# AFNO block on one core: the second DFT in products of 64 rows, the inverse on quarters of the array, the remainder evacuated once a chunk and moved by DMA

## The chip, the core and the metric

The kernel runs on one core of a Trainium2 chip. The metric is the device time of one execution in microseconds; times here are in microseconds where no other unit stands.

## What is computed

A block of 4096 positions and 640 channels: adaptive layer norm, a spectral mixer (AFNO) with residual, adaptive layer norm, a gated feed-forward layer with residual. The change concerns the mixer alone:

```python
Xf = jnp.fft.rfft2(x, axes=(1, 2))                   # x: (1, 1, 4096, 640)
z = Xf.reshape(B, H, Wf, NB, BS)                     # NB = 4 blocks of BS = 160 channels
hr = zr @ w1[0] - zi @ w1[1] + b1[0]                 # per block; einsum in the source
hi = zi @ w1[0] + zr @ w1[1] + b1[1]
hr = hr * (hr > 0); hi = hi * (hi > 0)
or_ = hr @ w2[0] - hi @ w2[1] + b2[0]
oi_ = hi @ w2[0] + hr @ w2[1] + b2[1]
...                                                  # soft shrink of both with lam = 0.01
return jnp.fft.irfft2(or_ + 1j * oi_, s=(H, W), axes=(1, 2))
```

## The kernel before

The transform of length 4096 is split into 128 x 32 (N1 x N2). A first DFT over N1 (`dft_a`, line 439) runs over eight pieces of the input, and its results are written to DRAM (`s1`, `write_s1`, line 355). The frequencies are then worked through in eight chunks `ch` (`NCH`, in the order `ORDER`), each of 512 frequencies in four groups `j`. A chunk is loaded by `load_g` (lines 308 and 311; the first chunk partly by `move_g`, line 316) into `gs[ch]`, its twiddled second DFT is `tb`.

For each chunk there are five second DFTs, `stage_b(ch, t)` (line 600): t = 0 to 3 for the first 128 channels of the four blocks, t = 4 for the remaining 32 channels of all four together (the remainder). `evac_b` takes a result from PSUM into a high and a low part `z` (ACT line 607, DVE line 608); `evac_rh` and `evac_rl` take the remainder into `rz`, 32 rows at a time (ACT line 630, DVE line 640). `stage_l1(ch, b)` (lines 661 and 674) is the first mixing layer of block b, `stage_l2` (line 711) the second, into `tts`. `move_x` (line 731) regroups `tts` by DMA into `xx`, `shrink_parts` (lines 737 and 738) and `shrink` are the soft shrink, `shrink_high` (line 752) and `shrink_low` (line 757) split it, and `stage_i` (lines 768 to 770) is the inverse of the second DFT, whose result is evacuated at line 771 and written to `s2` in DRAM by POOL's queue (line 772). The last chunk's inverse is apart (`inverse_last`, line 825), in f32 on 64 rows.

Matmuls with parts are fp32r in three products (high by high, low by high, high by low); `stage_b`, `dft_a`, `inverse_last` and the sums over `ones` are f32, and each of these products has two records in the trace.

The order is written out by hand (`manual_schedule`): what stands first in the program is issued first on its engine. The chunks run in 32 steps `p = 4 * ch + b`; step p has `stage_l1(p)`, one or two `stage_b`, `stage_l2(p - 1)`, `stage_i(p - 7)` and the elementwise work around them. A step with b = 1 has the remainder of the next chunk. `nc.sync` is the DMA queue of SP, in order; it carries the writes to `s1`, `load_g`, `load_tb`, the constants `idn`, `tx`, `bx`, the `move_x` and the loads for the modulation sums (`mod_load`). PSUM has eight banks: `p1`, `p2`, `p3` in pairs and `bank0(i)`, two single ones. Behind the chunks come `first_mm` (lines 983 to 988) and the feed-forward layer.

```python
for b, tag in ((0, None), (4, None), (1, "p2")):      # before the first step
    stage_b(0, b, tag)
...
for b in range(2):
    evac_b(0, b)
    evac_r(0, b)
```

Of the kernel before, what the change touches and what calls it, by code (L numbers as in the profile page):

```python
# [13 lines left out]
P = 128  # L14
# [32 lines left out]
def constants():  # L47
# [8 lines left out]
    fa = np.zeros((N1, 128))  # L56
# [30 lines left out]
    rows = lambda a: a.reshape(a.shape[0], 4, 8, 4, -1).transpose(0, 2, 3, 1, 4).reshape(a.shape[0], 128, -1)  # L87
    tb = rows(tb.transpose(0, 3, 1, 2, 4, 5, 6)).reshape(8, 4, 128, 128)[ORDER].reshape(32, 128, 128)
# [24 lines left out]
    bm = bm.reshape(2, 128, 128)  # L113
    bi = bm[1].reshape(2, 64, 128)

    bx = np.tile(bm[1].reshape(2, 64, 128).transpose(1, 0, 2), (2, 1, 1)).reshape(128, 256)
    bmh, bml = _hl(bm)
    bm = np.stack([bmh, bml], axis=1)
    bm = np.ascontiguousarray(bm.transpose(2, 0, 1, 3)).reshape(128, 2 * 2 * 128)
# [12 lines left out]
    for n in range(4):  # L132
        for h in range(2):
            for r in range(2):
                for i in range(2):
                    m = 4 * (4 * ORDER[-1] + 2 * h + i)
                    ge[64 * i:64 * i + 64, n, 256 * h + 128 * r:256 * h + 128 * r + 128] = (
                        bi[r].reshape(64, 4, 32)[:, :, n] @ ga[n, m:m + 4])
        ge[:, n, 512:] = ga[n]
# [18 lines left out]
def layouts(given):  # L158
    out = {}
    for n in ("A_w1", "A_w2"):  # L160
        w = given[n].transpose(2, 0, 1, 3)
        rows = [w[128:160, ::1 - 2 * (q % 2)] for q in range(4)]
        out[n] = np.ascontiguousarray(np.stack([w[0:128], np.concatenate(rows)]))
# [10 lines left out]
def body(tc, x, w1, b1, w2, b2, wg, wu, wd, c, wm, k_fa, k_tb, k_tx, k_bm, k_bx, k_ga, k_ge, k_id, out, dbg=None):  # L174
# [27 lines left out]
    with ExitStack() as top:  # L202
# [3 lines left out]
        def bank0(i, shape, name):  # L206
            return ps.tile(shape, F32, tag=f"b{i % 2}", bufs=1, name=name)
# [30 lines left out]
        with ExitStack() as af:  # L238
# [4 lines left out]
            bm = wp.tile([P, 2, 2, 128], F32R, name="bm")  # L243
            tx = wp.tile([P, 2], F32, name="tx")
            lp = af.enter_context(tc.tile_pool(name="lp", bufs=1))
            fa = lp.tile([P, 128], F32, name="fa")
# [9 lines left out]
            def prep_weights(raw, wa, wb, wc, split):  # L256
# [11 lines left out]
                for o in range(2):  # L268
                    for oh, ol, n, src in parts(o):
# [6 lines left out]
                                 (wc, h, l, rr[:, o, :, e], 1.0 if o else sgn[:, 0:1])]  # L276
# [19 lines left out]
            def load_tb(ch):  # L296
                tb = lp.tile([P, 4, 128], F32, tag="tb", bufs=2, name=f"tb{ch}")
                nc.sync.dma_start(tb, k_tb[:, 4 * ch:4 * ch + 4])
                tbs[ch] = tb


            def load_g(ch, us=None):
# [3 lines left out]
                src = s1[f].rearrange("(u v) (q e j) d -> e u (v q) (j d)", u=4, e=e, q=4)[ch % e]  # L306
                if us is None:
                    nc.sync.dma_start(gs[ch].rearrange("p j d -> p (j d)"), src.rearrange("u r d -> r u d"))
                else:
                    for u in us:  # L310
                        nc.sync.dma_start(gs[ch][u:P:4].rearrange("p j d -> p (j d)"), src[u])


            def move_g(ch, t, i, dma):
                p = 64 * (t % 2) + 16 * i + t // 2
                dma.dma_start(gs[ch][p:p + 13:4], xas[t][64 * ch:64 * ch + 64:4, i])
# [23 lines left out]
            with tc.tile_pool(name="sp", bufs=1) as sp:  # L340
# [91 lines left out]
                def dft_a(t):  # L432

                    xnr = xas[t].rearrange("p a (b e) -> p a b e", b=NB)
                    for n, i in enumerate((0, 1, 2, 3, 4) if t < 7 else (4, 0, 1, 2, 3)):
                        j = 5 * t + n
                        pa = (bank0(j // 4, [P, 512], f"pa{t}_{i}") if j % 4 == 0
                              else ps.tile([P, 512], F32, tag=f"p{j % 4}", name=f"pa{t}_{i}"))
                        mm(pa, fa, xnr[:, i, :, 0:128] if i < 4 else xnr[:, :, :, 128:160], start=True, stop=True)
# [15 lines left out]
                for t in range(8):  # L455
# [5 lines left out]
                    if t == 6:  # L461

                        prep1 = prep_weights(raws[1], w1a, w1b, w1c, True)
# [34 lines left out]
            load_g(1, range(4))  # L498
# [23 lines left out]
            prep2 = prep_weights(raws[2], w2a, w2b, w2c, False)  # L522
# [64 lines left out]
            pbs = {}  # L587
# [3 lines left out]
            def width(ch):  # L591
                return 258 if ch == CE else 256

            def stage_b(ch, t, tag=None):
                g, tb = gs[ch], tbs[ch]
                pb = (ps.tile([P, 2, 256], F32, tag=tag, name=f"pb{ch}_{t}") if tag else
                      bank0(1 if t == 4 else 0, [P, 2, 256], f"pb{ch}_{t}"))
                col = slice(128 * t, 128 * t + 128)
                for j in range(4):
                    mm(pb[:, :, 64 * j:64 * j + 64], g[:, j, col], tb[:, j, :], start=True, stop=True)  # L600
                pbs[ch, t] = pb

            def evac_b(ch, t):
                pb = pbs[ch, t]
                z = lp.tile([P, 2, 2, 258], F32R, tag="z", bufs=4, name=f"z{ch}_{t}")
                zs[ch, t] = z
                act.activation(z[:, 0, :, 0:256], pb, AF.Identity, scale=ca1[:, t:t + 1])
                dve.scalar_tensor_tensor(z[:, 1, :, 0:256], pb, ca1[:, t:t + 1],
                                         f32(z[:, 0, :, 0:256]), op0=OP.mult, op1=OP.subtract)
                if ch == CE:  # L610
                    pool.tensor_copy(z[:, 0, :, 0:257:256], f32(edge[:, 0, t]))
                    pool.tensor_copy(z[:, 1, :, 0:257:256], f32(edge[:, 1, t]))
                    pool.tensor_copy(z[:, :, :, 257], zero[:, 0, 0])


            def evac_r(ch, b, part=None):
                if part != 1:
                    evac_rh(ch, b)
                if part != 0:
                    evac_rl(ch, b)  # L620
# [1918 lines left out]
```

## Time and profile before

| | |
|---|---|
| three runs, median (lowest to highest) | 1415.19 (1413.05 to 1418.73) |
| span of the profiled execution | 1409.5 |
| its own time beside the span | not given; the median of the runs is 5.7 above the span |
| input, layer norm, first DFT | to about 56 |
| chunks | about 56 to 306 |
| feed-forward layer | about 306 to the end |
| granted clock of TensorE | 1.00 in all stretches asked for |

A row of the time line has the start, the length, the engine, the line, the operation with its tiles, and how many equal instructions it merges; in square brackets is the idle time of the engine ahead of it and what ended it. `PEld` is TensorE's weight load, `SPq` the issuing of DMAs by SP. A row of a group has the count, the busy time, the mean of one in ns, and the idle time ahead. `64*128` is the part of the array that a matmul uses, rows by columns.

### The profile page before, as it was taken

The numbers are of one execution on the slowest core, as the hardware profiler recorded it, in microseconds if no ns is written. First come the engines' busy times: TensorE is split into PE (matmuls) and PEld (weight loads), VectorE is DVE, ScalarE is ACT, GpSimd is POOL, SyncE is SP. The second block draws the span as 40 slices with busy tenths as digits, with TensorE's granted clock in tenths as the row PEclk, the third lists the DMA queues.
The fourth block names the chain that finished last, engine by engine and source line by source line (L and its number), as shares of the span: only waits on it lengthen the run. The fifth ranks groups of instructions, "written<-read, shape, count | busy, mean of one in ns | idle before, by whom it ended". The sixth has DMA issues, their size and how long they took to land. (4 is left out here: it accounts for less than half of the span.)

```text
span 1409.5 us, 23754 instructions
## 1 busy us (share of the span) xinstructions
PE 1382.5 (98%) x8410; PEld 1310.7 (93%) x8410; DVE 1067.8 (76%) x1861; ACT 765.0 (54%) x1542; POOL 604.6 (43%) x683
## 2 busy tenths in 40 slices
PE   6899999999999999999999999999999999999998
PEld 2599999967999889899999999999999999999998
DVE  8889888889888888649787668678678757375644
ACT  6879999755555554436454345546164624262341
POOL 5700200157766594326445534447153624042241
PEclk9999999999999999999999999999999999999999
DMA  9876466675998897898877998696998668956634
GB/s 371 310 244 211 157 196 193 203 232 170 327 353 308 308 335 263 293 368 308 308 225 281 375 330 288 236 326 230 375 330 309 217 218 282 350 194 217 199 115 149
DMA packets 171016, 377.34 MB, mean 268 GB/s; under 512 B 22193, under 2 KB 81649, under 8 KB 168882
## 3 DMA queue, kind: packets, MB, share of 16 engines
q1 hardware_dynamic: 161794, 359.28, 73.6%
q0 software_dynamic: 6800, 13.93, 3.1%
q10 hardware_dynamic: 2304, 2.62, 0.5%
q8 instruction: 66, 1.08, 0.3%
q14 instruction: 52, 0.43, 0.1%
HBM read 269.48 MB, written 96.80 MB: 260 GB/s over the span
## 5 line engine op out<-in xcount | busy, mean ns | idle before, releaser
L1442 DVE TENSOR_TENSOR wb<-r,wb 128x768 fp32r<-128x768 f32 (+3 forms) x170 | 170.4, 1013 | 13.5 <-ACT wb L1435 13.3
L2050 PE MATMUL pw<-h,wt 128*128 128x384 f32 x412 | 139.3, 338 | 0.6 <-ACT s_y L2069 0.6
L2052 PE MATMUL pw<-h,wt 128*128 128x384 f32 x412 | 138.3, 336 | 0.0
L2051 PE MATMUL pw<-h,wt 128*128 128x384 f32 x412 | 138.1, 335 | 0.0
L1435 ACT ACTIVATE wb<-r 128x768 fp32r<-128x768 f32 (+3 forms) x168 | 104.5, 639 | 56.3 <-PE pw L2063 41.7
L2351 PE MATMUL pc<-wq,L 128*128 128x320 f32 x846 | 132.7, 309 | 0.9 <-DMA wq<-wqd 0.9
L2110 POOL TENSOR_TENSOR sg<-s_x,sg 128x384 f32<-128x384 f32 x24 | 30.0, 1250 | 234.5 <-DVE s_x L2076 234.5
L2351 PEld LDWEIGHTS pc<-wq,L 128*128 128x128 f32 x846 | 126.3, 188 | 1.1 <-DVE x L2308 1.1
L2130 DVE TENSOR_TENSOR L<-sg,L 128x384 fp32r<-128x384 f32 x144 | 101.0, 725 | 27.7 <-ACT L L2126 27.2
L2069 ACT ACTIVATE s_x<-pw 128x384 f32<-128x384 f32 x52 | 25.6, 492 | 164.2 <-PE pw L2052 162.3
L2050 PE MATMUL pw<-h,wb 128*128 128x384 f32 x312 | 105.0, 336 | 0.0
L2051 PE MATMUL pw<-h,wb 128*128 128x384 f32 x312 | 104.4, 335 | 0.0
L2052 PE MATMUL pw<-h,wb 128*128 128x384 f32 x312 | 104.4, 335 | 0.0
L2121 POOL TENSOR_TENSOR sg<-sg,sg 128x384 f32<-128x384 f32 x72 | 91.9, 1276 | 23.4 <-DVE L L2130 20.0
L1973 PE MATMUL pg<-ht,wb 128*128 128x512 f32 x260 | 101.8, 392 | 0.0
L2351 PE MATMUL pe<-wq,L 128*128 128x320 f32 x648 | 101.7, 309 | 0.0
L1974 PE MATMUL pg<-ht,wb 128*128 128x512 f32 x260 | 101.3, 390 | 0.0
L1975 PE MATMUL pg<-ht,wb 128*128 128x512 f32 x260 | 101.2, 389 | 0.0
L2267 PE MATMUL pd<-wq,a 128*128 128x320 f32 x632 | 96.8, 310 | 0.0
L2351 PEld LDWEIGHTS pe<-wq,L 128*128 128x128 f32 x648 | 96.6, 188 | 0.0
L2267 PEld LDWEIGHTS pd<-wq,a 128*128 128x128 f32 x632 | 93.5, 188 | 0.5
L772 POOL DMA_DIRECT2D s<-co x28 | 15.7, 559 | 175.9 <-ACT co L771 175.9
(317 smaller groups left out, 3914.1 us busy)
## 6 DMA issues: line engine op xcount, KB each, us to landing
wq<-wqd SPq DMA_DIRECT2D x83, 640.0 KB, 6.1
wt<-td SPq DMA_DIRECT2D x103, 512.0 KB, 5.4
hs<-ho SPq DMA_DIRECT2D x52, 512.0 KB, 5.2
h<-hs SPq DMA_DIRECT2D x32, 768.0 KB, 7.9
td<-wt SPq DMA_DIRECT2D x25, 512.0 KB, 6.3
r<-in_B_w_gate_dram SPq DMA_DIRECT2D x24, 384.0 KB, 4.4
r<-in_B_w_up_dram SPq DMA_DIRECT2D x24, 384.0 KB, 4.3
xx<-tt SPq DMA_DIRECT2D x56, 160.0 KB, 3.3
```

The costliest lines, as they stand in the source:

```text
L1435: def high(ks, e=slice(0, c), copy=lambda o, i: act.activation(o, i, AF.Copy)):
L1442: dve.tensor_tensor(wbs[t, n][:, 1, ks, e], raw[t, n][:, ks, e], f32(wbs[t, n][:, 0, ks, e]), op=OP.subtract)
L1973: mm(b, wh, hh, start=(kk == 0), stop=False)
L1974: mm(b, wh, hl, start=False, stop=False)
L1975: mm(b, wl, hh, start=False, stop=(kk == 4))
L2050: mm(b, w(0, kp), a[:, kp, 0], start=start and kp == 0, stop=False, skip_group_check=not start)
L2051: mm(b, w(0, kp), a[:, kp, 1], start=False, stop=False, skip_group_check=not start)
L2052: mm(b, w(1, kp), a[:, kp, 0], start=False, stop=kp == 1, skip_group_check=not start)
L2121: pool.tensor_tensor(o, x, y, op=op)
L2130: dve.tensor_tensor(o[:, 1], raws[j], f32(o[:, 0]), op=OP.subtract)
L2267: mm(b[:, :320], l, m, start=start and i == 0, stop=stop and i == len(s) - 1)
L2351: mm(o[:, :320], ls[q][:, x, k], w[:, q, y], start=start and q == 0 and n == 0, stop=q == 1 and n == 2, skip_group_check=not start)
```

## The change

`stage_b` no longer multiplies all 128 rows by a matrix of 128 columns, half of it zeros. The rows of `gs` are ordered so that one frequency of each pair lies in rows 0 to 63 and the other in 64 to 127, and each group has two products of 64 rows with 64 columns, one for each half, which write to two banks of PSUM (`bb`, one tile of two banks that `bank0` now hands out too). The remainder (t = 4) is evacuated whole by two ACT and two DVE instructions into a tile `zr`, and `move_r` moves it by four DMAs on SP's queue into `rz`. `stage_i` is in f32 without splitting, as four products of 64 rows and 64 columns, each on a quarter of the array; it stands at p - 6, and its result is written by two DMAs of POOL instead of one. `move_x` needs one DMA for each tile instead of two, `load_g` always four. The load of `bm` moves from POOL's queue to SP's. In the first step the products of `z` stand ahead of those of `rz`.

```diff
+        bb = ps.tile([P, 2, 512], F32, tag="bb", bufs=1, name="bb")
-        def bank0(i, shape, name):
-            return ps.tile(shape, F32, tag=f"b{i % 2}", bufs=1, name=name)
+        def bank0(i):
+            return bb[:, i % 2]
...
-            def stage_b(ch, t, tag=None):
+            def stage_b(ch, t, two=None):
                 g, tb = gs[ch], tbs[ch]
-                pb = (ps.tile([P, 2, 256], F32, tag=tag, name=f"pb{ch}_{t}") if tag else
-                      bank0(1 if t == 4 else 0, [P, 2, 256], f"pb{ch}_{t}"))
+                out = [two[u] if two else bb[:, u] for u in range(2)]
+                out = [o[:, 0:256].rearrange("p (r e) -> p r e", r=2) for o in out]
                 col = slice(128 * t, 128 * t + 128)
                 for j in range(4):
-                    mm(pb[:, :, 64 * j:64 * j + 64], g[:, j, col], tb[:, j, :], start=True, stop=True)
+                    for u in range(2):
+                        k = slice(64 * u, 64 * u + 64)
+                        mm(out[u][:, :, 32 * j:32 * j + 32], g[k, j, col], tb[k, j, :], start=True, stop=True)
...
+            def evac_b(ch, t, two=None):
...
+                if t == 4:
+                    cuts = [(bb[:, :, 128 * r:128 * r + 128], slice(0, 2), r) for r in range(2)]
...
+                for pv, u, r in cuts:
+                    zh, zl = (v[:, u] if r is None else v[:, u, r, cols] for v in zv)
+                    act.activation(zh, pv, AF.Identity, scale=ca1[:, t:t + 1])
+                    dve.scalar_tensor_tensor(zl, pv, ca1[:, t:t + 1], f32(zh), op0=OP.mult, op1=OP.subtract)
...
+            def move_r(ch):
+                rzs[ch] = hp.tile([P, NB, 260], F32R, tag="rz", bufs=2, name=f"rz{ch}")
+                NN = width(ch)
+                for b in range(NB):
+                    nc.sync.dma_start(f32(rzs[ch][:, b, :NN]), f32(zs[ch, 4][32 * b:32 * b + 32, 0:4 * NN]).rearrange(
+                        "p (q e) -> p q e", q=4))
...
+                if not ch and not b:
+                    for o, n in ((0, 6), (1, 6), (2, 4)):
+                        products(o, 0, n)
...
             def move_x(ch, i):
-                for r in range(2):
-                    nc.sync.dma_start(xx[64 * r:64 * r + 64, :], tts[ch, q][64 * h:64 * h + 64, r, :])
+                nc.sync.dma_start(xx, tts[ch, u][64 * h:64 * h + 64])
...
             def stage_i(ch, i):
-                    mm(pi[:, :320], bm[:, kd, 0, :], xh[:, e], start=True, stop=False)
-                    mm(pi[:, :320], bm[:, kd, 0, :], xl[:, e], start=False, stop=False)
-                    mm(pi[:, :320], bm[:, kd, 1, :], xh[:, e], start=False, stop=True)
-                    act.activation(co[:, e], pi[:, :320], AF.Copy)
-                pool.dma_start(s2[4 * J:4 * J + 4].rearrange("k n d -> (k n) d"), co)
+                for e in range(2):
+                    for u in range(2):
+                        k = slice(64 * u, 64 * u + 64)
+                        mm(pi[u][64 * e:64 * e + 64, :320], bm[k, kd], xx[k, 320 * e:320 * e + 320], start=True, stop=True)
+                for u in range(2):
+                    act.activation(co[:, u], pi[u][:, :320], AF.Copy)
+                for e in range(2):
+                    pool.dma_start(rows[:, :, :, 320 * e:320 * e + 320].rearrange("u k n d -> (k n) u d"), co[64 * e:64 * e + 64])
...
-            for b, tag in ((0, None), (4, None), (1, "p2")):
-                stage_b(0, b, tag)
+            two = [ps.tile([P, 512], F32, tag="p2", name=f"pb0_{u}") for u in range(2)]
+            stage_b(0, 4)
+            stage_b(0, 0, two)
...
-            for b in range(2):
-                evac_b(0, b)
-                evac_r(0, b)
+            evac_b(0, 4)
+            move_r(0)
+            evac_b(0, 0, two)
+            stage_b(0, 1)
+            evac_b(0, 1)
...
-                on(stage_l1, p)
...
+                if todo and todo[0][1] == 4:
+                    q = todo.pop(0)
+                    stage_b(*q)
+                    evac_b(*q)
+                    move_r(q[0])
+                on(stage_l1, p)
...
-                on(stage_i, p - 7)
+                on(stage_i, p - 6)
...
-                    pool.dma_start(bm.rearrange("p a b c -> p (a b c)"), k_bm)
+                    nc.sync.dma_start(bm.rearrange("p a b -> p (a b)"), k_bm)
```

The order on three places, before and after. First SP's queue at the start of the chunks (`rz<-z` is `move_r`); before:

```order
L509 DMA tx<-in_k_tx_dram 128x2
L531 DMA bx<-in_k_bx_dram 128x256
L308 DMA g_898<-s 128x1x2560
L298 DMA tb_900<-in_k_tb_dram 128x512
L536 DMA wm_0_987<-in_w_mod_dram 128x640
```

and after:

```order
L507 DMA tx<-in_k_tx_dram 128x2
L529 DMA bx<-in_k_bx_dram 128x256
L633 DMA rz_662<-z_4_657 128x1x256 x4
L885 DMA bm<-in_k_bm_dram 128x128
L633 DMA rz_835<-z_4_830 128x1x256 x4
L309 DMA g_912<-s 32x1x2560 x4
```

The first chunk's remainder is moved behind bx, and with it behind all the writes to s1; the second chunk's stands ahead of the load of the third.

Second PE in the first step (`pl_0_o` are the three results of stage_l1); before:

```order
L661 MATMUL pl_0_0_685<-z_0_663,w1a 128x256 x3
L661 MATMUL pl_0_0_685<-z_0_663,w1b 128x256 x3
L661 MATMUL pl_0_0_685<-rz_666,w1c 128x256 x2
L661 MATMUL pl_0_1_699<-z_0_663,w1a 128x256 x3
L661 MATMUL pl_0_1_699<-z_0_663,w1b 128x256 x3
L661 MATMUL pl_0_1_699<-rz_666,w1c 128x256 x2
```

and after:

```order
L661 MATMUL pl_0_0_690<-z_0_667,w1a 128x256 x3
L661 MATMUL pl_0_0_690<-z_0_667,w1b 128x256 x3
L661 MATMUL pl_0_1_691<-z_0_667,w1a 128x256 x3
L661 MATMUL pl_0_1_691<-z_0_667,w1b 128x256 x3
L661 MATMUL pl_0_2_692<-z_0_667,w1a 128x256 x2
L661 MATMUL pl_0_2_692<-z_0_667,w1b 128x256 x2
L661 MATMUL pl_0_0_690<-rz_662,w1c 128x256 x2
L661 MATMUL pl_0_1_691<-rz_662,w1c 128x256 x2
```

The products with rz have moved behind the 16 with z; everything behind them on PE comes later still.

Third PE in a later step, where a block with b = 1 follows (`bb` is stage_b's result, `pi` stage_i's); before:

```order
L711 MATMUL pc_1_1_1617<-w2c,r_2_1_1483 128x320 x2
L768 MATMUL pi_0_1628<-xh_3_1503,bm 128x320
L769 MATMUL pi_0_1628<-xl_3_1504,bm 128x320
L770 MATMUL pi_0_1628<-xh_3_1503,bm 128x320
L768 MATMUL pi_1_1633<-xh_3_1503,bm 128x320
L769 MATMUL pi_1_1633<-xl_3_1504,bm 128x320
L770 MATMUL pi_1_1633<-xh_3_1503,bm 128x320
L661 MATMUL pl_3_0_1645<-z_3_1386,w1a 128x256 x3
```

and after, at a step's end ahead of one with b = 1:

```order
L713 MATMUL pc_3_1_1428<-w2c,r_1_3_1306 128x320 x2
L763 MATMUL pi_0_1439<-xx_2_1080,bm 64x320
L763 MATMUL pi_1_1440<-xx_2_1080,bm 64x320
L763 MATMUL pi_0_1439<-xx_2_1080,bm 64x320
L763 MATMUL pi_1_1440<-xx_2_1080,bm 64x320
L599 MATMUL bb<-tb_1360,g_1355 128x2x32 x8
L661 MATMUL pl_1_0_1479<-z_1_1228,w1a 128x256 x3
```

Six products of 128 rows have become four of 64, and the remainder's stage_b has moved ahead of stage_l1; the next stage_b into the same `bb` stands behind that stage_l1.

More of the change, by code (lines that the diff above doesn't have):

```diff
@@ L497, in body @@
                 write_s1(t, 1)
-            load_g(1, range(4))
+            load_g(1)
             load_tb(1)
@@ new lines, in stage_l1, with products @@
+                    pls.append(ps.tile([P, 512], F32, tag="p1", name=f"pl{ch}_{b}_{o}"))
+                cs = slice(512, 640)
+                seqs.append([(l[:, b, cs], m) for l, m in (
+                    (w1a, z[0][:, 0]), (w1a, z[1][:, 0]), (w1b, z[0][:, 1]),
+                    (w1b, z[1][:, 1]), (w1c, r[:, :NN]))])
+                pls.append(bank0(1) if 4 * ch + b > LAST else
+                           ps.tile([P, 512], F32, tag="p3", name=f"pl{ch}_{b}_2"))
+                def products(o, lo=0, hi=8):
+                    for i, (l, m) in enumerate(seqs[o]):
+                        if lo <= i < hi:
+                            mm(pls[o][:, :NN], l, m, start=(i == 0), stop=(i == len(seqs[o]) - 1))
@@ L908, in load_first @@
                 x2s[0] = x2
-            for f in (shrink, shrink_high, shrink_low):
-                on(f, LAST - 5)
-            on(stage_i, LAST - 6)
+            on(shrink, LAST - 5)
             for p in range(LAST + 1, NP):
```

224 lines of the change are left out of this document (83 added, 141 removed).

## The prediction

> **What bounds the kernel now.** I read the page's busy times, then the windows, then the groups and the time line of the stretch that the change touches. The page:
>
> ```profile
> PE 1382.5 (98%) x8410; PEld 1310.7 (93%) x8410; DVE 1067.8 (76%) x1861; ACT 765.0 (54%) x1542; POOL 604.6 (43%) x683
> ```
>
> The same by stage (busy time and count of PE, PEld, DVE, ACT, POOL, then granted clock, DMA share, GB/s):
>
> ```profile
> 58.50:84.76 26.26, 23.39 (x183) 22.57 (x182) 21.39 (x38) 19.66 (x43) 9.60 (x8) 1.00 0.99 362
> 84.76:284.00 199.24, 199.01 (x1541) 197.23 (x1539) 176.42 (x343) 179.62 (x373) 20.32 (x57) 1.00 0.60 192
> 306.00:1409.50 1103.50, 1092.98 (x6478) 1055.47 (x6475) 801.36 (x1303) 514.00 (x1040) 529.36 (x531) 1.00 0.80 277
> ```
>
> The first two rows are the AFNO chunks. From 84.76 on PE idles 0.2 us in 199: what the change adds to PE there is added to the end, and what it takes from ACT (90% busy) and DVE (89%) comes free only if PE waits for them, which it does not. Behind 306 both programs have the same instructions in the same order, so that stretch only shifts. In the first row the DMA engines are 99% busy; that decides the largest term below.
>
> Spacings, from PE's time line, are what PE pays for one piece of work; a row's busy time includes the latency of its last matmul:
>
> ```profile
> 71.60 0.52 PE L661 MATMUL pl<-z,w1a 128*128 128x256 f32 x3
> ...
> 74.08 1.95 PE L600 MATMUL pb<-tb,g 128*128 128x128 f32 x16
> 75.79 0.69 PE L711 MATMUL pc<-w2a,h 128*128 128x320 f32 x3
> ...
> 78.22 0.52 PE L661 MATMUL pl<-z,w1a 128*128 128x256 f32 x3
> ...
> 133.73 0.95 PE L327 MATMUL pmc<-ones,acc 128*128 128x1 f32 x8
> ...
> 137.21 0.31 PE L768 MATMUL pi<-xh,bm 128*128 128x320 f32 x1
> ...
> 138.09 0.51 PE L661 MATMUL pl<-z,w1a 128*128 128x256 f32 x3
> ```
>
> stage_l1 costs 74.08 - 71.60 = 2.48 (21 matmuls, 0.118 each), stage_l2 78.22 - 75.79 = 2.43 (16, 0.15 each), one stage_b 0.86 to 0.89 (the four f32 products are eight records, 0.11 each), stage_i 138.09 - 137.21 = 0.88 (six). The row of L327 moves one column and still starts every 0.10: there 128 weight columns set the pace, so stage_b's 0.11 is the weight load's price, with 128 moving columns behind it.
>
> **Start: the moved remainder.** Before, PE ran the first chunk like this:
>
> ```profile
> 55.84 2.92 PE L600 MATMUL pb<-tb,g 128*128 128x128 f32 x24 [1.43 <-DMA g<-xa]
> 58.51 0.60 PE L661 MATMUL pl<-z,w1a 128*128 128x256 f32 x3
> ...
> 59.99 0.48 PE L661 MATMUL pl<-rz,w1c 128*128 128x256 f32 x2 [0.52 <-DVE rz L640]
> ...
> 84.76 0.59 PE L661 MATMUL pl<-z,w1a 128*128 128x256 f32 x3
> ```
>
> rz came from ACT and DVE at 59.99; step 4 began at 84.76. Now rz comes by four DMAs on SP's queue, which the program puts behind bx. SP's queue before:
>
> ```profile
> 52.50 9.40 SPq L355 DMA_DIRECT2D s<-xa  x8
> 61.94 3.69 SPq L311 DMA_DIRECT2D g<-s  x4
> 65.69 0.57 SPq L298 DMA_DIRECT2D tb<-in_k_tb_dram  x1
> 66.30 11.38 SPq L355 DMA_DIRECT2D s<-xa  x10
> 77.72 1.37 SPq L508 DMA_DIRECT2D idn<-in_k_id_dram  x1
> ...
> 80.42 0.95 SPq L531 DMA_DIRECT2D bx<-in_k_bx_dram  x1
> 81.61 0.57 SPq L308 DMA_DIRECT2D g<-s  x1
> ```
>
> Nothing ahead of rz has gone, and the eighteen s1 writes are held by the transfers themselves (share 0.99), so rz is issued at about 81.5. From issue to landing, first bx's own, then the 56 xx moves between SBUF tiles (min, median, max):
>
> ```profile
> DMA to landing us min/median/max: 3.6/3.6/3.6
> ...
> DMA to landing us min/median/max: 2.4/3.3/4.8
> ```
>
> With 3.5, rz is there at 85.0. PE can do only 16 products of step 0 ahead of it (they stand first now), some 1.9 us, and then waits for about 23. Of what it did before 84.76 there remain 5 products (0.59), three stage_l1 (7.44), three stage_l2 (7.29) and six stage_b (5.3): 20.6, so step 4 starts at 105.6: **+20.9**. Landing 2.4 behind an issue at 80.7 gives +19; 4.8 behind one at 83, with 1 us of new waits, +24. Who waits for PE there has no other work for it; SP's next entry, bm (moved here from POOL), is needed only at step 6.
>
> After an idle stretch PE is slow. The DFT's matmuls, at its cold start and later:
>
> ```profile
> 7.98 9.09 PE L439 MATMUL pa<-xa,fa 128*128 128x512 f32 x14 [7.98 <-ACT xa L418]
> ...
> 46.56 2.74 PE L439 MATMUL pa<-xa,fa 128*128 128x512 f32 x6
> ```
>
> Later one starts every (2.74 - 0.59)/5 = 0.43; the first fourteen took 9.09 - 0.59 - 13 x 0.43 = 2.9 more than that. I take **+2.9** for the 23 us wait, with 0 as the other end, since no row shows PE behind a wait of that length in the middle.
>
> The Trainium skill ("TensorE: Matmul & The Clock Gate", Part 1) says that about 3.4 us of idleness halve PE's clock and that it comes back after one busy window of 3.4 us. By that the term would be an estimated 1.7 to 3.4, and the sum would move by about 1; the row stays.
>
> **Products on 64 rows.** The only rows with them are the last chunk's inverse:
>
> ```profile
> 284.81 1.35 PE L825 MATMUL pi<-tt,bx 64*128 64x320 f32 x8 [0.53 <-ACT co L771]
> 286.10 0.41 PE L768 MATMUL pi<-xh,bm 128*128 128x320 f32 x1
> 286.35 0.31 PE L769 MATMUL pi<-xl,bm 128*128 128x320 f32 x1
> ...
> 289.95 5.65 PE L983 MATMUL py<-tt,et 128*128 128x320 f32 x20
> ...
> 302.87 0.43 PE L988 MATMUL py<-cfrr,et 112*128 112x320 f32 x1
> 303.23 0.55 PE L825 MATMUL pi<-tt,bx 64*128 64x320 f32 x2
> ```
>
> An f32 matmul of 320 columns starts every (5.65 - 0.54)/19 = 0.27 (L983). Eight on 64 rows, four on each half, one after the other would take 7 x 0.27 + 0.43 = 2.3; they took 1.35 = 3 x 0.27 + 0.43 + 0.1. So the two halves run side by side, and the second half's do not wait for the first half's, which stand ahead of them. But PE empties when the shape changes: from 302.87 to 303.23 are 0.36, 0.27 of streaming and 0.09 of nothing, and then the weights of 0.11 are loaded in the open (303.23's first has 0.53 instead of 0.43). On the way out it is the same (286.10's 0.41 instead of 0.31, the next at 0.25 instead of 0.15).
>
> stage_b: per half eight records with 128 weight columns, 0.11 each: 0.88, as before; the moving side went from 128 to 64 columns, but it was not what set the pace. Going in, behind L661: 0.107 + 0.09 + 0.107 = 0.30 instead of 0.12, +0.185; going out 0.054 + 0.09 + 0.107 = 0.25 instead of 0.11, +0.14. In PE's order there are 36 such blocks behind the first; five follow a stage_i and save the way in: 36 x 0.325 - 5 x 0.185 = **+10.8**. Ends: 0 (if shapes change without a price in a full queue) and +16 (if 16 records need 0.15 more to be issued).
>
> stage_i: four f32 products, eight records, on four quarters, 0.27 each, 64 weight columns (0.054, half of 0.107). Two halves at a time, in order in each, would take 4 x 0.27 = 1.07; all four quarters at a time 2 x 0.27 = 0.53. No row has two column halves. Between the ends I take three times 0.27 = 0.80: in a half the second quarter's first starts behind the first quarter's second, beside which it can run. In: +0.13; out: +0.20. So 1.13 instead of 0.88, 28 times: **+7.0**. Ends: 0.86 (-0.6 in all) and 1.40 (+14.6).
>
> **One pair of banks.** stage_b of the remainder used another bank than the next; now both fill bb whole, and in steps with b = 1 the second stage_b needs both evacuations of the first. ACT reaches these behind its copies and shrink_parts:
>
> ```profile
> L630 ACT ACTIVATE rz<-pb,ca 32x256 fp32r<-32x256 f32 x50 | 23.3, 466 | 0.8
> L771 ACT ACTIVATE co<-pi 128x320 f32<-128x320 f32 x52 | 21.1, 435 | 3.6 <-PE pi L770 3.3
> L738 ACT ACTIVATE xx<-xx,nlam 128x640 f32<-128x640 f32 x23 | 19.1, 832 | 0.7
> ...
> L640 DVE SCALAR_TENSOR_TENSOR rz<-pb,ca,rz 32x256 fp32r<-32x256 f32 x54 | 26.1, 483 | 6.3 <-ACT rz L630 5.3
> ```
>
> From stage_i's end: copies and parts 0.2 + 0.87 + 1.66, two evacuations of 0.47, DVE's last of 0.48: 4.2. PE is ready after stage_b and stage_l1, 3.7. So 0.5 for six chunks, **+3**; ends 0 and +6.
>
> **At nothing.** Per chunk six of eight L630 (0.47) and L640 (0.48), and in stage_i the high and low parts, leave ACT and DVE; that is some 40 us on each, hidden by PE. SP's later rz moves come three steps (20 us) ahead of their use; behind them stand only weights for mod_add. move_x issues four DMAs instead of eight, load_g four instead of one, ahead by two steps. POOL issues two s2 writes instead of one and is idle there.
>
> Sum: 20.9 + 2.9 + 10.8 + 7.0 + 3 = 44.6 on a span of 1409.5: 1454. The page gives a span alone; the runs' median of 1415.2 lies 5.7 above it, so I say **1460**.
>
> **Rivals.** (1) All four quarters at once: 7.6 less, 1452. The eight L825 speak for tiles that go their own way. The Trainium skill ("TensorEngine Tiling (Array Packing)", Key Properties) has this: 64x64 makes four tiles, and different tiles load and multiply in parallel. (2) Products keep the program's order across tiles: then only neighbours overlap, stage_i takes 5 x 0.27 + 0.33 = 1.68, +22 instead of +7, 1475. The Trainium skill ("TensorE: Matmul & The Clock Gate", Part 3) says so: matmuls start and end strictly in order. The 1.35 of the eight L825 speaks against it (2.3 by that rule). (3) The remainder comes without a stall, because SP passes the writes sooner: without 23.8, 1436. It would have to land by 62; share 0.99 speaks against it. (4) Shapes change for free in a full queue: stage_b at 0 and stage_i at 0.80 against 0.88, -2.2 in all, so 1440. (5) Faster: PE looks past a waiting or emptying instruction to the next one of another tile, as the L825 hint, so that neither the wait for rz nor a change of shape costs, and two halves of quarters save 0.35 x 28 = 9.8: 1405. It decides if PE passes a semaphore's wait. At 59.99 it did not: PE idled 0.52 for rz while ready products of z stood behind.
>
> **Chances.** Forecast 0.42, (1) 0.27, (2) 0.12, (3) 0.06, (4) 0.10, (5) 0.03. The range reaches from rival (3) and (4) to the forecast with its upper ends and (2): 1434 to 1478. A change under 0.5% (7 us) can't be told from none; 7 us would need nearly all terms to fall: faster 0.03, same 0.03, slower 0.94.
>
> **What would show it.** The first rz move issued at 81 to 82 and PE idle from about 62 to 85, then matmuls at double spacing for some us; step 4 near 108. In a step, L599 and L763 each with a weight load 0.09 behind the end of the last stream; L763 from first start to last 0.54, 0.8 or 1.07. ACT and DVE under 75% busy between 110 and 300. The forecast is wrong if rz lands before 65, or if the steps are not longer than 6.8 on average.

## The result, and the profile after

| kernel | median, us | lowest to highest | ratio to before (95% interval) |
|---|---|---|---|
| before | 1414.5 | 1413.1 to 1418.7 | |
| after | 1598.9 | 1594.8 to 1603.3 | 1.1312 (1.129 to 1.1335) |

The change makes the kernel 184 us slower. The forecast of 1460 (1434 to 1478) had the sign right and the size four times too small. The page of after, with the profiled span, the busy times, PE's granted clock in 40 slices and the shares of the chain that ended last:

```profile
span 1593.0 us, 24417 instructions
PE 1441.0 (90%) x8786; PEld 1320.7 (83%) x8786; DVE 1017.8 (64%) x1790; ACT 723.0 (45%) x1471; POOL 607.7 (38%) x711
PEclk9769898998899999999999999999999999999999
PE 69%; DVE 12%; DMA 10%; issue 4%; ACT 3%; POOL 2%; SPq 1%; ACTq 0%; DVEq 0%; POOLq 0%
```

PE was 98% busy and is 90%. DVE and DMA now hold 22% of the chain that ended last, where the page of before gives every engine but PE 0%. By stage, cut at the first product of step 0, of step 4, of step 31 and at the first transpose of the feed-forward (columns as in the prediction):

```profile
68.06:121.53 53.47, 29.86 (x230) 28.01 (x228) 15.46 (x29) 14.26 (x32) 7.25 (x6) 0.67 0.47 165
121.53:346.30 224.77, 205.98 (x1773) 182.07 (x1771) 136.13 (x266) 138.66 (x300) 33.35 (x80) 0.95 0.57 169
346.30:389.08 42.78, 33.54 (x150) 21.51 (x146) 25.51 (x50) 11.97 (x24) 12.88 (x23) 0.88 0.51 154
389.08:1593.00 1203.92, 1123.05 (x6491) 1066.09 (x6490) 790.18 (x1303) 514.25 (x1042) 517.42 (x530) 0.99 0.74 254
```

Every stage lost, and in every one PE idles. The same cuts of both traces, from the starts of the instructions:

```
                                   before    after    lost
start of step 4                      84.8    121.5    36.8
steps 4 to 31                       190.1    224.8    34.7
step 31 to the feed-forward          30.9     42.8    11.9
feed-forward                       1103.8   1203.9   100.1
sum                                1409.5   1593.0   183.5
```

More than half is lost in the feed-forward, in which not one instruction was added (six products of the last inverse fall behind the cut, among the first transposes). What PE waits for, longest first (engine, tile and line, what released it; total us, times, longest):

```profile
PE bb L2031 <- DVE s_v L2057: 37.0, 36, 2.5
PE pl L661 <- DMA rz<-z: 23.6, 1, 23.6
PE bb L599 <- DMA xx<-tt: 13.1, 2, 7.1
PE bb L2332 <- DVE s_v L2057: 12.6, 12, 2.3
...
PE pg L1954 <- ACT gbb L1617: 7.7, 1, 7.7
PE py L969 <- DMA cfrm<-s: 5.5, 1, 5.5
PE bb L599 <- DMA g<-xa: 4.7, 1, 4.7
```

Of these rows only the second was forecast. The first and fourth are in the feed-forward, on bb. The third names xx, but the program's waits at that place are for g and tb of the next chunk: the transfer that came last is named, not the one whose data PE needs.

### The profile page after: what moved, and what is told of

It reads as the page before. It is cut to its first block, busy times and chain, and to the rows that moved or that the text cites. A ratio compares the mean times of both kernels' runs of the same rounds, so it can differ in the third digit from the quotient of the medians.

```text
span 1593.0 us, 24417 instructions
## 1 busy us (share of the span) xinstructions
PE 1441.0 (90%) x8786; PEld 1320.7 (83%) x8786; DVE 1017.8 (64%) x1790; ACT 723.0 (45%) x1471; POOL 607.7 (38%) x711
## 3 DMA queue, kind: packets, MB, share of 16 engines
q8 instruction: 69, 1.13, 0.3%
## 4 chain that ended last, share of the span: by engine, by line
PE 69%; DVE 12%; DMA 10%; issue 4%; ACT 3%; POOL 2%; SPq 1%; ACTq 0%; DVEq 0%; POOLq 0%
PE bb L2332 5%; PE pc L2332 4%; PE pe L2332 4%; PE pl L661 4%; PE pc L713 4%; PE pw L2031 4%; PE pw L2033 4%; PE pw L2032 4%; PE bb L2031 4%; PE pd L2248 4%; PE bb L2033 3%; PE bb L2032 3%; PE bb L599 2%; DMA g<-s 2%; PE pg L1956 2%
## 5 line engine op out<-in xcount | busy, mean ns | idle before, releaser
L2050 ACT ACTIVATE s_x<-bb 128x384 f32<-128x384 f32 x52 | 25.6, 493 | 232.2 <-PE bb L2033 226.3
L2332 PE MATMUL bb<-wq,L 128*128 128x320 f32 x522 | 92.4, 312 | 13.9 <-DVE s_v L2057 11.6
L2332 PEld LDWEIGHTS bb<-wq,L 128*128 128x128 f32 x522 | 79.4, 188 | 18.7 <-DVE s_v L2057 15.1
L1954 PE MATMUL pg<-ht,wb 128*128 128x512 f32 x195 | 77.2, 396 | 7.7 <-ACT gbb L1617 7.7
L2332 PE MATMUL pe<-wq,L 128*128 128x320 f32 x504 | 82.1, 310 | 0.0
L2031 PE MATMUL bb<-h,wb 128*128 128x384 f32 x104 | 40.2, 387 | 44.0 <-DVE s_v L2057 37.0
L2289 DVE TENSOR_TENSOR x<-x,bb 128x320 f32<-128x320 f32 x100 | 48.4, 484 | 47.9 <-PE bb L2332 27.8
L2332 PE MATMUL pc<-wq,L 128*128 128x320 f32 x468 | 78.0, 313 | 0.0
L1955 PE MATMUL pg<-ht,wb 128*128 128x512 f32 x195 | 76.7, 393 | 0.0
L1956 PE MATMUL pg<-ht,wb 128*128 128x512 f32 x195 | 76.6, 393 | 0.0
L2332 PEld LDWEIGHTS pe<-wq,L 128*128 128x128 f32 x504 | 76.3, 189 | 0.0
L2107 ACT ACTIVATE L<-sg 128x384 fp32r<-128x384 f32 x144 | 69.4, 517 | 5.0 <-POOL sg L2102 2.6
L2332 PEld LDWEIGHTS pc<-wq,L 128*128 128x128 f32 x468 | 71.6, 190 | 0.0
L2031 PE MATMUL pw<-h,wb 128*128 128x384 f32 x208 | 70.3, 338 | 0.0
```

What stands on the lines that cost most here:

```text
L1954: mm(b, wh, hh, start=(kk == 0), stop=False)
L1955: mm(b, wh, hl, start=False, stop=False)
L1956: mm(b, wl, hh, start=False, stop=(kk == 4))
L2031: mm(b, w(0, kp), a[:, kp, 0], start=start and kp == 0, stop=False, skip_group_check=not start)
L2332: mm(o[:, :320], ls[q][:, x, k], w[:, q, y], start=start and q == 0 and n == 0, stop=q == 1 and n == 2, skip_group_check=not start)
```

## The experiments

**Two tiles of one bank in the feed-forward.** bank0 now hands out halves of one tile, bb. By the semaphore waits in the program after, PE waits 145 times in the feed-forward, ahead of a write into one bank of bb, for DVE's last reading of the other bank, and 7 times for one of the same bank; of its waits for ACT's readings of bb, 155 of 161 are for the same bank. The time line of after shows such a place:

```profile
1003.82 0.34 PE L2044 MATMUL bb<-h,wb 128*128 128x384 f32 x1
...
1005.25 0.55 DVE L2057 TENSOR_TENSOR s_v<-bb,s_v 128x384 f32<-128x384 f32 x1
...
1005.85 1.15 PE L2332 MATMUL bb<-wq,L 128*128 128x320 f32 x6 [1.70 <-DVE s_v L2057]
```

The down product L2332 writes the other bank than the one that L2057 reads, and stands 1.70 us until DVE has read it.

```diff
-        bb = ps.tile([P, 2, 512], F32, tag="bb", bufs=1, name="bb")
+        bs = ExitStack()
+        bp = bs.enter_context(tc.tile_pool(name="bp", bufs=1, space=PSUM))
+        bb = bp.tile([P, 2, 512], F32, tag="bb", bufs=1, name="bb")
...
+        bs.close()
+        bp = top.enter_context(tc.tile_pool(name="bq", bufs=1, space=PSUM))
+        def bank0(i):
+            return bp.tile([P, 512], F32, tag=f"b{i % 2}", bufs=1, name="bf")
         with ExitStack() as ff:
```

> The kernel after, with the pair of banks given back when the AFNO stage ends: the feed-forward takes two tiles of one bank each from a pool of its own, as the kernel before did. The AFNO stage is untouched. Theory A (the feed-forward's 100 us are waits of a product into one bank for the DVE's last reading of the other, because both banks are one tile): the feed-forward from its first transpose to the end goes from 1203.9 back to 1103.8 within 5 us, the row of L2031 that waits for s_v (37.0 us) goes, and the time falls to 1490 to 1505. Theory B (the feed-forward is slower because it starts in another state: weights and tokens that arrive late, a lower granted clock after a disturbed stage): the time stays above 1580. A mixture lies between.

Measured: 1519.6, ratio 1.0767 (1.0734 to 1.0801), 79 us less than after. The feed-forward takes 1127.5, not 1203.9. The groups of L2031 on wb, of after and then of this kernel (last columns: idle time ahead and its releasers):

```profile
L2031 PE MATMUL bb<-h,wb 128*128 128x384 f32 x104 | 40.2, 387 | 44.0 <-DVE s_v L2057 37.0 <-DVE sgr L1923 4.1 <-DVE x L2289 2.9
```

```profile
L2039 PE MATMUL bf<-h,wb 128*128 128x384 f32 x104 | 35.2, 339 | 0.1
```

The idle 44.0 became 0.1, and this program has no wait for DVE's reading of the other bank in the feed-forward. Theory A holds for 76 of the feed-forward's 100 us; 24 are left, 19 of them within its first 45 us, and need another cause.

**The converse: before with one tile.** The feed-forward of before takes its two banks as halves of one tile. The banks of the AFNO stage come from a pool of their own, which is closed there; nothing else is changed.

```diff
-            return ps.tile(shape, F32, tag=f"b{i % 2}", bufs=1, name=name)
+            return bp.tile(shape, F32, tag=f"b{i % 2}", bufs=1, name=name)
...
+        bs.close()
+        bp = top.enter_context(tc.tile_pool(name="bq", bufs=1, space=PSUM))
+        bb = bp.tile([P, 2, 512], F32, tag="bb", bufs=1, name="bb")
+
+        def bank0(i, shape, name):
+            return bb[:, i % 2]
```

> The converse: the kernel before, whose feed-forward alone now takes its two banks as the halves of one tile. Theory A: some 95 to 105 us slower than the kernel before, so 1508 to 1520, with waits of L2050 and L2351 for s_v that were not there. Theory B: within 5 us of 1414.

Measured: 1499.1, ratio 1.0614 (1.0596 to 1.0632), +87, a little under the forecast. The waits of after appear in the kernel before:

```profile
PE bb L2061 <- DVE s_v L2087: 36.8, 36, 2.5
PE bb L2362 <- DVE s_v L2087: 12.6, 12, 2.3
```

The same 36 and 12 waits, the same 49 us. Here the AFNO stage is untouched, so no late start, late weight or slow clock is needed for them. The rows on bb come to some 61 us in all. Of the other 26, the granted clock accounts for an estimated 14: between 311.9 and 1049.1 it is at half in seven stretches of 3.4 to 6.9 us, in which PE works for 27.5 us, while before had 1.00 in all of its feed-forward. The rest was not resolved.

**Where g lands.** PE needs a new g every four steps; in after two of these came 6 to 7 us late. In a stretch in which g is the bulk of the traffic, the windows show the share of the sixteen DMA engines at work (last but one column), first of after, then of before:

```profile
157.00:159.50 2.50, 2.01 (x17) 1.25 (x16) 2.37 (x5) 0.78 (x4) 0.00 (x0) 1.00 0.25 107
```

```profile
84.00:86.50 2.50, 2.50 (x24) 2.50 (x22) 1.96 (x5) 1.98 (x5) 0.00 (x0) 1.00 0.96 373
```

A load of g is 128 packets of 10,240 bytes. In before they lie within 4 to 7 us, 8 to 14 at a time; in after within 13 to 17 us, 3.4 to 3.9 at a time, in every chunk from the second on. The change gave the source the order q, v, whose outer dimension has 4 steps and doesn't merge with the inner one. This cuts the load by q instead of by u, so that the outer dimension (v) has 8:

```diff
+                if ch > 1:
+                    for q in range(4):
+                        nc.sync.dma_start(gs[ch][32 * q:32 * q + 32]..., src[:, q].rearrange("u v r -> v u r"))
+                    return
                 for u in us:
                     nc.sync.dma_start(gs[ch][u:P:4]..., src[u])
```

> The kernel after, with the loads of g for the chunks from 2 on cut the other way: still four transfers of 32 rows, but each goes to 32 neighbouring partitions and not to every fourth one. Theory C (the rows of one such transfer lie on few of the sixteen DMA engines, so a load of g takes 17 to 20 us): the waits of 7.07 us at step 9 and of 6 us at step 21 go and with them the slow clock behind them, 14 to 18 us less, 1581 to 1586. Theory D (the load is late because it is issued behind the moves of xx and shares the engines with them, whatever its partitions): within 4 us of 1599.

Measured: 1576.0, ratio 1.1165 (1.1148 to 1.1182), 23 us less, more than the forecast 14 to 18. The row "L599 <- DMA xx<-tt" is gone. The share in this kernel while g lands:

```profile
149.00:150.50 1.50, 1.50 (x15) 1.50 (x14) 0.60 (x1) 1.47 (x4) 0.79 (x2) 1.00 0.50 212
```

Four steps gave 0.25, eight give 0.50, 32 gave 0.96. The Trainium skill ("DMA: Bandwidth & Descriptors", on why a DMA increments its semaphore by 16) has the rule: a transfer runs on the largest number of engines up to 16 that divides the slowest dimension of both sides. The three shares agree with it.

**The first remainder on ACT's queue.** The forecast's own term. In after, rz is issued at 90.2, behind the s1 writes and bx.

```diff
-            def move_r(ch):
+            def move_r(ch, q=nc.sync):
...
-            move_r(0)
+            move_r(0, nc.scalar)
```

> The kernel after, with the four moves of the first chunk's remainder issued by ACT and not by SP, so that they stand behind the evacuation alone and not behind SP's writes of s1. Theory E (the first 23.6 us wait is SP's queue): the moves are issued some 15 us sooner, the wait falls to 5 to 9 us, and with the slow clock that follows it 15 to 20 us are saved: 1579 to 1584. Theory F (the moves would wait for something else by then, or the next stage only waits for the other weights of the first layer): less than 8 us are saved.

Measured: 1600.1, ratio 1.1325 (1.13 to 1.1349): nothing gained. The moves on ACT's queue (count; ns min, median, max; first and last start):

```profile
L633 ACTq DMA_DIRECT2D rz<-z x4: 550/554/707, 89.1 to 93.9; - x4
ACT z L620: 29.3, 1
```

They still start at 89.1, and now ACT stands 29.3 us behind them, so that step 0 itself starts at 95.5 instead of 68.1. Theory F holds in that the moves waited for something else; that ACT itself would then stand, neither theory had. In the program each transfer that SP or ACT issues first waits until the one eight places before it, of SP and ACT together, has landed; ahead of rz these are the s1 writes. Another queue of the same kind doesn't pass them.

**The first remainder on POOL's queue**, whose transfers are counted apart:

```diff
-            move_r(0)
+            move_r(0, pool)
```

> The kernel after, with the first chunk's four remainder moves issued by POOL. On ACT they had issued at 89.1 us too, because each transfer there first waits for the one eight places before it, an s1 write of SP's queue, to land; POOL's transfers have counters of their own, and those are free by then. Theory E (SP's transfers hold the move back, by the queue or by the counters): the moves issue near 66 us and land by 72, step 1 starts at 76 to 80 instead of 98.7, and 15 to 20 us are saved: 1579 to 1584. Theory F (what comes next, g of chunk 2 or the weights of the second layer, is late in its turn): step 1 is early all the same, but less than 8 us are left at step 9.

Measured: 1582.2, ratio 1.1176 (1.1144 to 1.1208), 16.7 us less. Step 1 starts at 73.4 instead of 98.7, 25 us sooner. Of these 13 are left at step 4 and 15 at step 9. So theory E holds, and a part of theory F: the next wait takes some of it back (it is shown with the four repairs below).

**The last chunk's writes.** inverse_last writes s2 with an outer dimension of 2 (u). By the same rule these run on two engines: while they are under way in after, from 375.2 to 378.0, the share is 0.13. In after, POOL's four (ns, first and last start, and the times from issue to landing):

```profile
L825 POOL DMA_DIRECT2D s<-cz x4: 798/818/890, 391.0 to 411.5; - x4
DMA to landing us min/median/max: 6.2/6.4/6.7
```

In before they were issued from 307.8 to 309.7 and landed in 2.2 to 2.4.

```diff
-                (pool if hf else nc.scalar).dma_start(s2_rows(NCH - 1, i)[:, :, :, e].rearrange("u k n d -> u (k n) d"), co[:, e])
+                for u in range(2):
+                    (pool if hf else nc.scalar).dma_start(s2_rows(NCH - 1, i)[u, :, :, e]..., co[64 * u:64 * u + 64, e])
```

> The kernel after, with each of the eight s2 writes of the last chunk (inverse_last) made in two transfers of 64 rows, one for each u, and not in one whose outer dimension is 2. Theory G (a transfer is spread over as many DMA engines as its outer dimension has steps, so these writes use two of sixteen; ACT's four then last from 361 to 378, and POOL's four hold its queue for 21 us, so that the gate gbb and the first down weights of the feed-forward come late): each write lands in 2 to 3 us instead of 6.5, the 19 us that the feed-forward loses in its first 45 us go but for 3 or 4, the AFNO tail of 42.8 us shortens by 6 to 10, and the time falls by 20 to 28, to 1571 to 1579. Theory H (the feed-forward starts badly because of the shared banks or of what the late AFNO stage leaves behind): less than 8 us are saved.

Measured: 1572.2, ratio 1.1125 (1.1088 to 1.1163), 26.7 us less, inside theory G's range. POOL's, now eight:

```profile
L826 POOL DMA_DIRECT2D s<-cz x8: 532/532/797, 386.7 to 390.6; - x8
DMA to landing us min/median/max: 2.0/2.1/2.5
```

They hold POOL for 4 us, not 21, its first product of the down weights (L1524 in after) starts at 404.8 instead of 425.5, and PE's wait of 7.7 us for gbb is gone. The profiled execution was the longest of the four (1580.5): it shows 6.7 us less in the tail and 10.0 in the feed-forward, so not all of the 26.7 is seen in a trace.

**Number of transfers or their spread.** Before made one transfer of each g, after makes four. This gives before four, by u, with source rows that merge to 32 steps:

```diff
-            def load_g(ch, us=None):
+            def load_g(ch, us=range(4)):
```

> The kernel before, with every load of g made in four transfers of 32 rows to every fourth partition, as its first two chunks do it already; its source rows merge into one dimension of 32 steps. Theory G (spread over the engines by the outer dimension): all sixteen engines take part, so the time stays within 5 us of 1412. Rival (four transfers in place of one fill the queue and its counters, so that later ones wait): 10 us or more slower, with waits of L600 for g or tb.

Measured: 1412.7 against 1413.5, ratio 0.9993 (0.9977 to 1.0009). Four transfers cost nothing; the spread does.

**Four repairs together** (two tiles from the end of the last second DFT on, g by q from chunk 1 on, the last writes by 64 rows, the first remainder on POOL):

> The kernel after with four repairs together: two tiles of one bank from the end of the last second DFT on (tail and feed-forward), g from chunk 1 on to neighbouring partitions, the last chunk's s2 writes by 64 rows, the first remainder moves on POOL. If the four losses are separate: 79 + 23 + 24 + 17 us less, 1450 to 1465. If they hide one another, the time stays above 1480. What is then left over 1412 is the price of the change's own steps.

Measured: 1453.0, ratio 1.0274 (1.0247 to 1.03). Singly the four gave 79.3 + 23.0 + 26.7 + 16.7 = 145.7; together 145.9. The first two reach a little further here than singly, and the medians are good to some 3 us, so the agreement to 0.2 is luck; but the losses are separate in the main, and 39 us are left. By stage, in the profiled execution (+40.9): 20.3 at the start of step 3, 15.5 in steps 3 to 28, -1.4 in the last three, 3.2 in the tail, 3.3 in the feed-forward. The start, from this kernel's time line:

```profile
63.10 1.98 PE L608 MATMUL bb<-tb,g 64*128 64x64 f32 x16 [5.45 <-DMA g<-xa]
...
90.54 0.89 DVE L724 TENSOR_TENSOR tt<-pc,b2t 128x320 f32<-128x320 f32 x2 [7.53 <-DMA s<-xa]
...
92.90 1.97 PE L608 MATMUL bb<-tb,g 64*128 64x64 f32 x16 [6.33 <-DVE z L630]
```

The first g is 5.4 us late, and at step 2 DVE waits 7.5 us for the s1 writes (tt takes the memory that they read); z stands behind tt in DVE's order, and PE behind z. That is what took back a part of the remainder's gain.

**Rows of g in natural order.** To spread every load of g, the first too, over up to 32 steps (the rows of tb and of move_g are put in the same order):

```diff
-                src = s1[f].rearrange("(u v) (q e j) d -> e u q v (j d)", u=4, e=e, q=4)[ch % e]
+                src = s1[f].rearrange("n (q e j) d -> e q n (j d)", e=e, q=4)[ch % e]
+                for q in range(4):
+                    nc.sync.dma_start(gs[ch][32 * q + lo:32 * q + hi]..., src[q, lo:hi])
```

> The four repairs, and the rows of g in the order 32q + n2 (tb and tx reordered with them), so that each transfer of g, the first chunk's too, has one outer dimension of up to 32 steps on both sides. Theory G (engines by the outer dimension): the packets of 10,240 bytes start at some 20 to 40 in a us, not 8 as in the kernel after; the first g, which still came 5.4 us late in the four repairs, lands in time, step 0 starts at 60 to 62 instead of 69.1, SP's s1 writes end sooner and with them the 6.3 us wait of step 2: 10 to 16 us less than 1453, so 1437 to 1443. Rival (the start is held by SP's number of transfers and their counters: eight for the first g now, three before): no gain or a loss there, 1450 to 1460.

Measured: 1453.6, ratio 1.0284 (1.0256 to 1.0312), no gain. The spread came (the share in a load's window is below), the time didn't:

```profile
100.00:104.00 4.00, 4.00 (x40) 3.87 (x38) 1.32 (x3) 2.06 (x5) 0.00 (x0) 0.90 0.97 203
```

All engines are at work, at 203 GB/s where before had 373 with the same share: a packet of g takes some 0.7 us instead of 0.45. Step 0 starts at 72.2, later than 69.1. The rival was right about the time; whether by the count of the transfers, as it said, or by these slow packets is open.

**Fewer changes of tile shape.** The step that remains, from the time line of the four repairs:

```profile
285.18 0.28 PE L670 MATMUL pl<-rz,w1c 128*128 128x256 f32 x1
285.39 1.11 PE L608 MATMUL bb<-tb,g 64*128 64x64 f32 x16
286.43 0.70 PE L722 MATMUL pc<-w2a,h 128*128 128x320 f32 x3
...
288.98 0.77 PE L772 MATMUL pi<-xx,bm 64*64 64x320 f32 x8
289.68 0.63 PE L670 MATMUL pl<-z,w1a 128*128 128x256 f32 x3
```

A normal step takes 6.95 instead of 6.60. Here the second DFT is put behind the second layer, beside the inverse, in all steps from 4 on:

```diff
                 on(stage_l1, p)
-                for q in todo:
+                for q in todo if p < 4 else ():
                     stage_b(*q)
                     evac_b(*q)
...
                     on(stage_l2, p - 1)
+                for q in todo if p > 3 else ():
+                    stage_b(*q)
+                    evac_b(*q)
                 on(stage_i, p - 6)
```

> The four repairs, with the second DFT of each step from 4 on moved behind the second layer, directly ahead of the inverse on quarters, so that PE changes its tile shape once in and once out in a step and not twice. Theory S (each change of shape costs: weight loads held for 0.2 us on the way in, 0.2 and more on the way out): a normal step falls from 6.95 to 6.55 to 6.75, 24 steps, 5 to 10 us less than 1453. Theory T (the steps are longer for another reason, evacuation or buffers): within 3 us of 1453, or slower because z now comes later than the first layer wants it.

Measured: 1453.1, ratio 1.028 (1.0253 to 1.0306), as the four repairs: theory T's time. Yet a normal step did fall, to 6.75 to 6.78, as theory S had it. The gain went into the steps b=0, whose second DFT is now followed at once by the next chunk's: from step 8 to 9 it takes 8.83 instead of 7.99, from 24 to 25 8.83 instead of 8.01. Together with the natural rows:

> Both of the two edits before: 15 to 25 us less than 1453 if theories G and S hold, 1428 to 1438, still above 1412.

Measured: 1456.9, ratio 1.0302 (1.0273 to 1.033), no more than either alone, and far from 1428 to 1438.

**The same, but not in the steps b=0**, so that no two second DFTs follow each other (against the kernel of the move beside the inverse, without the natural rows):

```diff
-                for q in todo if p < 4 else ():
+                for q in todo if p < 4 or b == 0 else ():
...
-                for q in todo if p > 3 else ():
+                for q in todo if p > 3 and b else ():
```

> The four repairs, with the second DFT moved beside the inverse as in e10, but not in the steps b=0, where it stays behind the first layer, so that no two second DFTs follow each other. Theory S (each change of tile shape costs 0.2 us) with the pair of banks (two second DFTs in a row wait 1.0 us for the evacuation of the one pair): normal steps 6.75 as in e10 and 6.95 in b=0 itself; the wait of 1.0 us, which e10 only carried from step b=1 into step b=0, goes; 1.4 to 1.8 us a chunk, six chunks: 8 to 11 us less than the four repairs, 1442 to 1446. Theory T (the time of a step is set by something else): within 3 us of 1453.

Measured: 1446.8, ratio 1.0256 (1.0239 to 1.0273), 6 us less than the four repairs, short of the 8 to 11. PE's waits from 105 to 290, of the four repairs and of this kernel:

```profile
PE bb L608 <- DVE z L630: 5.0, 5, 1.0
```

```profile
PE bb L608 <- DVE tt L724: 0.4, 1, 0.4
PE pl L670 <- ACT co L774: 0.4, 2, 0.2
```

Five waits of 1.0 us, one a chunk, are gone, and normal steps stay at 6.75. The missing part is in steps that became longer: 9.73 instead of 8.60 from 16 to 17, 8.54 instead of 7.99 from 8 to 9, 7.33 instead of 6.92 from 15 to 16. In the first of these the inverse takes 1.48 instead of 0.77, beside POOL's work for the edges; that this work is the cause was not shown. This is the best version with the change, and it is still 36 us slower than before.

## Why the prediction was right or wrong, point by point

- **The wait for the remainder (+20.9): right in its place and nearly in its length (23.6), too small in sum.** Step 4 starts 36.8 later, not 20.9 + 2.9. rz was there at 95.45 and not at 85.0, and behind it came 26.1 us of work and not 20.6; the wait has the forecast length because both its ends came some 10 us later than forecast, which is luck. The step of the working that failed is "Nothing ahead of rz has gone, ... so rz is issued at about 81.5": it went out at 90.2, and PE had it 5.3 later instead of 3.5. Ahead of it the loads of g for the second chunk are issued in 6.0 us (before 3.7) and the ten s1 writes behind them in 15.2 (before 11.4), since each waits for the one eight places before it; in the four repairs, where this g runs on eight engines, the same ten writes are issued in 10.5. The first g came late too (4.7), which no term held. Moving rz to a queue with counters of its own gave back 16.7.
- **The slow clock (+2.9): right in kind, and not only there.** Behind the long wait, two windows of after (last but two columns: PEclk):

```profile
99.00:102.50 3.50, 3.50 (x17) 3.50 (x18) 2.88 (x5) 2.39 (x5) 0.00 (x0) 0.50 0.02 5
102.50:105.00 2.50, 2.50 (x25) 2.21 (x24) 1.15 (x3) 1.51 (x4) 0.00 (x0) 0.77 0.00 0
```

  From 95.45 to 103.50 products start every 0.213 us, half speed, about 4 us lost. The clock falls again behind the waits at steps 9 (0.50 from 166 to 170) and 21. It was already low before the long wait, behind the 4.7 us for the first g (0.52 from 62.3 to 71.9).
- **stage_b on 64 rows (+0.325 a block): right.** In the four repairs 1.13 us lie between the end of the first layer's spacing and the second layer's first product (285.30 to 286.43), 0.80 before: +0.33. That it is the change of shape is shown by the move beside the inverse: one change in and out less in a step, 0.20 less.
- **stage_i on quarters (+0.25): wrong, rival (1) was right.** First to last start took 0.34 us and the block 0.75 to 0.80, where 0.54 to 1.07 had been asked for first to last: all four quarters run at once. So the block costs about what it did, and a step 0.35 more, not 0.575.
- **One pair of banks (0.5 in steps b=1): right in kind, twice as long, 1.0**, and shown by the last experiment. But only the AFNO stage was looked at. "Behind 306 both programs have the same instructions in the same order, so that stretch only shifts" is the step that failed most: the order was the same (but for the six products named above) and the waits were not. The same pair of banks cost 79 to 87 us there, in two experiments from both sides. Comparing the order of instructions can't show this; comparing whom each one waits for would have.
- **At nothing: "load_g four instead of one, ahead by two steps".** Wrong by 23: not the number (four transfers in before cost 0) but the outer dimension of 4.
- **The last chunk's writes** had no term. POOL was called idle beside the chunks' writes; here its four writes held it for 21 us ahead of the first down weights. 27 us.
- **ACT and DVE** fell as forecast: 60% and 57% busy from 110 to 300, under the 75% asked for, and it gained nothing, as forecast.

Rivals (2) to (5) fell: the order was not kept across tiles, the remainder did stall, a change of shape does cost, and PE did not look past the wait. In rival (2) the 2.3 is eight records one after the other; with neighbours overlapping across the halves it is 6 x 0.27 + 0.43 = 2.05, which the 1.35 excludes just as well. Of the 184 us, 129 (79 + 23 + 27) were in three places that were put at nothing or not looked at. Of the other 55, 16.7 came back with the remainder's queue and 15.5 are in steps 3 to 28 of the four repairs, both of terms that were worked out; the start costs 20.3 more, much of it for waits (g, the s1 writes) that no term held.

## What to carry to other kernels

When buffers are merged into one tile, list for each later user which instruction it now waits for; the same order of instructions says nothing about that. When a transfer's layout changes, look at the outer dimension of both sides after merging: 2, 4 or 8 steps there mean that many engines at work, and the share of the DMA engines in a window where it runs alone shows it at once. A wait taken away is worth what the next one leaves: 25 us at step 1 were 13 at step 4.

## What was not expected of the hardware

- Four f32 products on the four 64x64 quarters, eight records of 320 columns, took 0.77 us from first start to last end, what two records after each other take (0.34 + 0.43).
- Full use of the DMA engines is not full rate: share 0.97 with 203 GB/s against 0.96 with 373, for loads of g of the same size with the rows in another order. Why is open: the loads cut by q also go to 32 neighbouring partitions, on eight engines, and there a packet took 0.39 us.
- After a wait of 23.6 us PE ran at half speed for 8.0 us of uninterrupted work. The Trainium skill ("TensorE: Matmul & The Clock Gate", Part 1) gives one busy window of some 3.4 us for the return; the trace shows more than twice that.
